# Fold products in groups of eight, and zero fills moved behind the first unit's fifth step

## The chip, the cores and the metric

One core of a Trainium2 chip runs the whole program. The metric is the device time of one execution in microseconds; the kernel before took 965.82 us (median of three runs, 963.59 to 968.89). TensorE, VectorE, ScalarE and GpSimd each work through their own list of instructions in order; SyncE issues most DMAs, GpSimd the zero fills and the indexed writes. In the profile they are PE (its weight loads PEld), DVE, ACT, POOL and SP.

## The reference

Three layers in a row on 2304 tokens of width 512.

```python
# attention, 4 batches x 8 heads, 576 tokens, 32 landmarks (means of 18 rows)
A = sm(q, k_lm); Bm = sm(q_lm, k_lm); C = sm(q_lm, k)
Z = Bm.T / (norm1(Bm) * norminf(Bm) + 1e-6)
for _ in range(6):
    Z = 2 * Z - Z @ Bm @ Z
x = (A @ Z @ C @ v)                      # then heads side by side: 2304 x 512
# dense layer, 512 -> 2048 -> 512
h = x @ w_in; g = h * tanh(softplus(h)); x = g @ w_out
# eight experts, 512 -> 1024 -> 512, the best two of each token
logits = x @ w_gate + softplus(x @ w_noise) * noise
for e in range(8):                       # weights: softmax over the token's two
    out[mask] += top2_w * (relu(x[mask] @ w1[e]) @ w2[e])
```

## The kernel before

The tokens go through in eight units of 288, two per batch of the attention. `w_in` is never multiplied by the attention's output itself: per batch, the 32 landmark rows of each of the eight heads (`WT`, 64 x 32 per head, the product of `Z`, `C` and `v`) are multiplied into `w_in` first, which gives a 256 x 2048 matrix. This is **the fold** (`fold`, lines 680 to 713). It works in four blocks `fb` of 512 columns. For each block and each half `hg` (four heads), four products with 64 rows of `w_in`, 32 columns of weights and 512 columns of output run on TensorE (line 700), each in a quarter of the output partitions of one bank of tag g. ScalarE then copies the bank to `gt` in the matmul format (line 707), and VectorE writes what the rounding left over (line 709), so that later products are made of three parts. `w_in` comes as 64-bit integers holding doubles; `conv_in` converts it (`widen`, lines 599 to 603) in batch 0 and stores the result, and `reload_in` loads it again for batches 1 to 3 into six `win` buffers.

**The dense layer** is 64 steps, `hidden(s)`, eight per unit: step s makes 256 hidden columns of unit s // 8. A hidden step is twelve products into the one `ps_h` buffer (line 733, tile `gt` of block (s % 8) // 2); ScalarE copies it out (line 746), then come a minimum on VectorE (753), four activations (755 to 761), a VectorE product (763), and the parts `gh` (ScalarE, 768) and `gl` (VectorE, 771). Then come the step's 24 down products (788 to 790) into the unit's four accumulators (tag acc, four banks in all). "Down step 16" below is the point at which the down products of steps 0 to 15 are through, that is, batch 0's two units. `conv_out` loads the 16 chunks of `w_out` into two alternating buffers, widens them (tiles `raw` and `t`, line 599 on) and splits each (660 on ScalarE, 662 on VectorE).

**The attention** of batch b (`attention`) begins when some steps of the batch before are through. It loads kT and qT for two groups of heads and v, reduces kT and qT to landmarks (line 327), iterates Z (548 to 556) and ends in the W products (568), which VectorE copies into `WT` (571).

**Routing** (`route`) follows each unit: ScalarE copies the accumulators to `yT` (839, one buffer), VectorE transposes them into `rr` (851, one buffer), TensorE makes the gate products (866), VectorE ranks the experts in some forty small instructions, and GpSimd scatters each token's row to its slots in HBM (1012). The slots of the first round are filled with zeros first: `zeros` writes a zero tile (812) and issues 24 fills from GpSimd's queue (282), in three zones of rows per expert (288, 288, 64): eight fills of 96 x 3 x 516 floats for either large zone, eight of 64 x 516 for the small one. Unit 0's `route` waits for zone 0 to be filled, unit 1's for zone 1, unit 2's for zone 2.

Last come **the experts**, in jobs of 384 or 256 slots: gather and transpose, 12 products up and three per block down, and an indexed add to `out` (1185).

**The order of the work** is made by a planner, `Order.run`. Each part of the kernel is a generator that asks for an engine, a buffer or an event. Whenever an engine is free in the planner's clock, the ready request with the smallest due time is written down as the next instruction of that engine, with costs given by hand:

```python
yield op("T", 1.06)      # one fold group, planned cost in us
yield wait(event); tk = yield get(ring, n)
```

So a wait in this code decides where later instructions stand; on the chip an instruction waits only for the data and the buffers that it touches.

Of the kernel before, what the change touches and what calls it, by code (L numbers as in the profile page):

```python
# [6 lines left out]
F32 = mybir.dt.float32  # L7
# [5 lines left out]
OP = mybir.AluOpType  # L13
# [5 lines left out]
LM, SEG = 32, 18  # L19
# [167 lines left out]
def op(engine, cost, late=0.0):  # L187
    return ("op", engine, cost, late)


def wait(event):
    return ("wait", event)


def get(ring, n=1):
    return ("get", ring, n)
# [18 lines left out]
class Kern:  # L215
# [76 lines left out]
    def attention(self, b):  # L292
# [249 lines left out]
        for it in range(6):  # L542
            tk = yield get(self.r_g)
# [25 lines left out]
        for a in range(2):  # L569
            yield op("V", 0.13)  # L570
            V.tensor_copy(
                WT.rearrange("p (g a) l -> p g a l", a=2)[:, :, a, :], w[a][:, : 2 * LM].rearrange("p (g l) -> p g l", g=2)
            )
# [106 lines left out]
    def fold(self):  # L680

        o, V, A, T = self.o, self.V, self.A, self.T
        for b in range(B):
            yield wait(self.got_WT[b])
            for fb in range(4):
# [3 lines left out]
                tw = {}  # L689
                for hg in range(2):  # L690
                    for c in (2 * hg, 2 * hg + 1):
                        yield wait(self.got_win[b, fb, c])
                        tw[c] = self.t_win[fb, c]
                    tk = yield get(self.r_g)
                    p = self.bank()
                    yield op("T", 1.06)
                    for h in range(4):
                        r = slice(64 * (h % 2), 64 * (h % 2) + 64)
                        c = 2 * hg + h // 2
                        T.matmul(  # L700
                            p[32 * h : 32 * h + 32, :], self.WT[b][r, c, :], self.win[fb, c][r].bitcast(F32),
                            start=True, stop=True,
                        )
                    for c in (2 * hg, 2 * hg + 1):
                        o.put(self.r_win, tw[c])
                    yield op("A", ca(512))
                    A.copy(gt[:, 0, hg, :], p)
                    yield op("V", cv(512))
                    V.tensor_tensor(out=gt[:, 1, hg, :], in0=p, in1=gt[:, 0, hg, :].bitcast(F32), op=OP.subtract)
                    o.put(self.r_g, tk)  # L710
# [94 lines left out]
    def zeros(self):  # L805


        yield wait(self.downed[2])
# [19 lines left out]
    def route(self, u, acc, ta):  # L828
# [28 lines left out]
        if u < len(self.filled):  # L857
            yield wait(self.filled[u])
# [557 lines left out]
def lay_out(q, k, v, moe_w_in, moe_w_out, moe2_w_gate, moe2_w_noise, moe2_noise, moe2_w1, moe2_w2):  # L1416
# [11 lines left out]
    wi = c(moe_w_in.reshape(4, 128, 4, 512).transpose(2, 0, 1, 3)).reshape(16, 128, 512).view(np.int64)  # L1428
# [27 lines left out]
```

## Time and profile before

| | |
|---|---|
| median of three runs | 965.82 us (963.59, 965.82, 968.89) |
| profiled execution: device time | 968.66 us |
| its span, first to last instruction | 966.8 us, 18134 instructions |
| mean granted TensorE clock | 0.984 |
| fold, line 700: TensorE | 34.2 us busy in 256 matmuls |
| zero fills of the slots: DMA issues | 16 of 580.5 KB, and eight small ones |

Each run is one execution; the profile is of a further one. Busy time of an engine is the time in which at least one of its instructions is in flight. Matmuls are pipelined, so rows of the timeline overlap: their starts tell the pace. A row's bracket says how long the engine had been idle before it, and whose end released it. A line number is that of the function that issued it; loads all go through line 287 and zero fills through 282, so for these the tile's name tells which it is.

### The profile page before, as it was taken

The numbers are of one execution on the slowest core, as the hardware profiler recorded it, in microseconds if no ns is written. First come the engines' busy times: TensorE is split into PE (matmuls) and PEld (weight loads), VectorE is DVE, ScalarE is ACT, GpSimd is POOL, SyncE is SP. The second block draws the span as 40 slices with busy tenths as digits, with TensorE's granted clock in tenths as the row PEclk, the third lists the DMA queues.
The fourth block names the chain that finished last, engine by engine and source line by source line (L and its number), as shares of the span: only waits on it lengthen the run. The fifth ranks groups of instructions, "written<-read, shape, count | busy, mean of one in ns | idle before, by whom it ended". The sixth has DMA issues, their size and how long they took to land. (4 is left out here: it accounts for less than half of the span.)

```text
span 966.8 us, 18134 instructions
## 1 busy us (share of the span) xinstructions
PE 914.0 (95%) x7135; PEld 799.1 (83%) x7135; DVE 625.7 (65%) x1519; ACT 457.6 (47%) x825; POOL 136.4 (14%) x129
## 2 busy tenths in 40 slices
PE   9979768999999998999999989999999999999995
PEld 7767656878886877889898979899989899999984
DVE  6999689566986669486958466646565555445411
ACT  2247655667766686588853233333333223323210
POOL 0002100223101200202020412101121011111102
PEclk9989989999999999999999999999999999999998
DMA  8677950565406410323243667666556355464103
GB/s 303 198 256 255 360 209 3 152 192 173 194 7 200 164 53 2 115 67 86 58 153 91 153 191 162 148 169 143 135 118 158 109 111 125 98 165 94 17 3 51
DMA packets 70075, 131.62 MB, mean 136 GB/s; under 512 B 13696, under 2 KB 34784, under 8 KB 69984
## 3 DMA queue, kind: packets, MB, share of 16 engines
q1 hardware_dynamic: 56960, 96.16, 32.6%
q0 software_dynamic: 13024, 34.25, 15.1%
q8 instruction: 58, 0.95, 0.4%
q14 instruction: 33, 0.27, 0.1%
HBM read 91.94 MB, written 39.48 MB: 136 GB/s over the span
## 5 line engine op out<-in xcount | busy, mean ns | idle before, releaser
L1151 PE MATMUL ps_up<-xh,mw 128*128 128x256 f32 (+1 forms) x1024 | 265.5, 312 | 2.8 <-ACT mw L1039 2.1
L1151 PEld LDWEIGHTS ps_up<-xh,mw 128*128 128x128 f32 x1024 | 183.1, 189 | 15.5 <-ACT mw L1039 2.5
L1160 ACT ACTIVATE gh<-ps_up 128x384 fp32r<-128x384 f32 (+1 forms) x128 | 56.1, 438 | 285.7 <-PE ps_acc L1173 161.6
L1162 DVE SCALAR_TENSOR_TENSOR gl<-ps_up,gh 128x384 fp32r<-128x384 f32 (+1 forms) x128 | 62.7, 490 | 170.1 <-ACT gh L1160 169.9
L788 PE MATMUL ps_acc<-gh,wo 128*128 128x288 f32 x512 | 159.2, 311 | 5.3 <-ACT gh L768 5.0
L1151 PE MATMUL ps_up<-xl,mw 128*128 128x384 f32 (+1 forms) x512 | 159.3, 311 | 0.0
L789 PE MATMUL ps_acc<-gl,wo 128*128 128x288 f32 x512 | 153.2, 299 | 2.8 <-DVE gl L771 2.8
L790 PE MATMUL ps_acc<-gh,wo 128*128 128x288 f32 x512 | 152.7, 298 | 0.2 <-DVE wo L662 0.2
L733 PE MATMUL ps_h<-ah,gt 128*128 128x288 f32 x512 | 127.3, 306 | 15.7 <-ACT mh L746 15.2
L1172 PE MATMUL ps_acc<-mw,gh 128*128 128x512 f32 x320 | 126.5, 395 | 0.0
L1173 PE MATMUL ps_acc<-mw,gh 128*128 128x512 f32 x320 | 126.4, 395 | 0.0
L1174 PE MATMUL ps_acc<-mw,gl 128*128 128x512 f32 x320 | 125.8, 393 | 0.0
L1185 POOL DMA_INDIRECT out<-yp,off x40 | 67.0, 1674 | 376.9 <-DVE yp L1181 278.3
L788 PEld LDWEIGHTS ps_acc<-gh,wo 128*128 128x128 f32 x512 | 97.9, 191 | 25.5 <-issue 13.2
L733 PEld LDWEIGHTS ps_h<-ah,gt 128*128 128x128 f32 x512 | 90.0, 191 | 32.5 <-ACT mh L746 21.5
L1151 PEld LDWEIGHTS ps_up<-xl,mw 128*128 128x128 f32 x512 | 96.7, 189 | 10.0
L789 PEld LDWEIGHTS ps_acc<-gl,wo 128*128 128x128 f32 x512 | 98.0, 191 | 3.8 <-DVE gl L771 3.8
L1041 DVE TENSOR_TENSOR mw<-mraw,mw 128x1024 fp32r<-128x1024 f32 x72 | 87.8, 1223 | 18.5 <-ACT mw L1039 17.9
L790 PEld LDWEIGHTS ps_acc<-gh,wo 128*128 128x128 f32 x512 | 97.9, 191 | 0.4 <-DVE wo L662 0.4
L1012 POOL DMA_INDIRECT slots<-rr,sl x48 | 47.7, 994 | 336.4 <-DVE rr L1008 319.4
L1039 ACT CAST mw<-mraw 128x1024 fp32r<-128x1024 f32 x72 | 74.6, 1042 | 3.4 <-DMA mraw<-in_ew 3.4
L733 PE MATMUL ps_h<-al,gt 128*128 128x288 f32 x256 | 76.0, 297 | 0.0
(189 smaller groups left out, 1384.9 us busy)
## 6 DMA issues: line engine op xcount, KB each, us to landing
mraw<-in_ew SPq DMA_DIRECT2D x72, 512.0 KB, 4.1
win<-win_d SPq DMA_DIRECT2D x48, 256.0 KB, 3.4
xg<-slots SPq DMA_DIRECT2D x160, 64.0 KB, 3.1
slots<-zero POOLq DMA_DIRECT2D x16, 580.5 KB, 20.0
raw<-in_w_in SPq DMA_DIRECT2D x16, 512.0 KB, 4.7
raw<-in_w_out SPq DMA_DIRECT2D x16, 512.0 KB, 6.3
kT<-in_kT SPq DMA_DIRECT2D x8, 576.0 KB, 6.9
qT<-in_qT SPq DMA_DIRECT2D x8, 576.0 KB, 7.3
```

The source lines that it names most:

```text
L733: T.matmul(hp[:, i, :U], gt[:, x, hg, n : n + 128], AT[y][:, hg, :], start=k == 0, stop=k == 5)
L788: T.matmul(acc[c][:, :U], hi[:, n], gh[:, i], start=f + i == 0, stop=False)
L789: T.matmul(acc[c][:, :U], hi[:, n], gl[:, i], start=False, stop=False)
L790: T.matmul(acc[c][:, :U], lo[:, n], gh[:, i], start=False, stop=f + i == NF - 1)
L1039: self.A.copy(w[:, 0], raw)
L1041: self.V.tensor_tensor(out=w[:, 1], in0=raw, in1=w[:, 0].bitcast(F32), op=OP.subtract)
L1151: T.matmul(h[:, :n], w[:, i, 128 * c : 128 * c + 128], x[j][:, c, :n], start=k == 0, stop=k == 11)
L1162: self.V.scalar_tensor_tensor(out=gl[:, :n], in0=hp[:, :n], scalar=0.0, in1=gh[:, :n].bitcast(F32), op0=OP.max, op1=OP.subtract)
L1172: T.matmul(a, g[0][:, n], w[:, 0, 512:], start=first, stop=False)
L1173: T.matmul(a, g[0][:, n], w[:, 1, 512:], start=False, stop=False)
L1174: T.matmul(a, g[1][:, n], w[:, 0, 512:], start=False, stop=last)
L1185: st = self.G.indirect_dma_start(out=self.out[:, :], out_offset=bass.IndirectOffsetOnAxis(ap=off[:, b : b + 1], axis=0), in_=y, in_offset= ...
```

## The change

- The fold takes both halves of a block together: eight products of 64 x 32 into two banks. Of half 1 the two row halves change places (`(h ^ hg) % 2`), so that over each 32 columns one product uses rows 0 to 63 and one rows 64 to 127. The planner's cost of the group is 1.15 instead of two times 1.06; a group waits for all four `win` chunks and for two banks of tag g.
- For this, `w_in` is laid out with the row halves of chunks 2 and 3 exchanged (on the host), and `WT` is filled by two copies of 128 partitions and four of 64 per batch instead of two.
- The zero fills begin when down step 5 is planned (`downed[4]`) instead of down step 3 (`downed[2]`).
- Unit 0's `route` waits until all 24 fills have been issued; units 1 and 2 wait for none.

```diff
--- before.py
+++ after.py
@@ -568,9 +568,11 @@
                     T.matmul(w[a][R[h], LM * hg : LM * hg + LM], X[H[h], hg, LM:], R5[H[h], hg, :], start=True, stop=True)
         for a in range(2):
             yield op("V", 0.13)
-            V.tensor_copy(
-                WT.rearrange("p (g a) l -> p g a l", a=2)[:, :, a, :], w[a][:, : 2 * LM].rearrange("p (g l) -> p g l", g=2)
-            )
+            V.tensor_copy(WT[:, a], w[a][:, :LM])
+
+            for h in range(2):
+                yield op("V", 0.1)
+                V.tensor_copy(WT[R[1 - h], 2 + a], w[a][R[h], LM : 2 * LM])
         o.put(self.r_g, tk, 2)
         o.set(self.got_WT[b])
         for hg in range(2):
@@ -687,27 +689,29 @@
                 self.t_gt[b, fb] = yield get(self.r_gt)
                 self.gt[b, fb] = gt = self.gp.tile([128, 2, 2, 512], F32R, name="gt", tag="gt", bufs=4)
                 tw = {}
-                for hg in range(2):
-                    for c in (2 * hg, 2 * hg + 1):
-                        yield wait(self.got_win[b, fb, c])
-                        tw[c] = self.t_win[fb, c]
-                    tk = yield get(self.r_g)
-                    p = self.bank()
-                    yield op("T", 1.06)
-                    for h in range(4):
-                        r = slice(64 * (h % 2), 64 * (h % 2) + 64)
+                for c in range(4):
+                    yield wait(self.got_win[b, fb, c])
+                    tw[c] = self.t_win[fb, c]
+                tk = yield get(self.r_g, 2)
+                p = [self.bank() for _ in range(2)]
+
+                yield op("T", 1.15)
+                for h in range(4):
+                    for hg in range(2):
+                        r = slice(64 * ((h ^ hg) % 2), 64 * ((h ^ hg) % 2) + 64)
                         c = 2 * hg + h // 2
                         T.matmul(
-                            p[32 * h : 32 * h + 32, :], self.WT[b][r, c, :], self.win[fb, c][r].bitcast(F32),
+                            p[hg][32 * h : 32 * h + 32, :], self.WT[b][r, c, :], self.win[fb, c][r].bitcast(F32),
                             start=True, stop=True,
                         )
-                    for c in (2 * hg, 2 * hg + 1):
-                        o.put(self.r_win, tw[c])
+                for c in range(4):
+                    o.put(self.r_win, tw[c])
+                for hg in range(2):
                     yield op("A", ca(512))
-                    A.copy(gt[:, 0, hg, :], p)
+                    A.copy(gt[:, 0, hg, :], p[hg])
                     yield op("V", cv(512))
-                    V.tensor_tensor(out=gt[:, 1, hg, :], in0=p, in1=gt[:, 0, hg, :].bitcast(F32), op=OP.subtract)
-                    o.put(self.r_g, tk)
+                    V.tensor_tensor(out=gt[:, 1, hg, :], in0=p[hg], in1=gt[:, 0, hg, :].bitcast(F32), op=OP.subtract)
+                    o.put(self.r_g, tk + hg)
                 o.set(self.got_gt[b, fb])
             o.put(self.r_wt, self.t_WT[b])
         o.set(self.folded)
@@ -805,7 +809,7 @@
     def zeros(self):
 
 
-        yield wait(self.downed[2])
+        yield wait(self.downed[4])
         tk = yield get(self.r_raw)
         zero = self.wp.tile([128, D + LW], F32, name="zero", tag="raw", bufs=2)
         yield op("V", 0.2)
@@ -854,8 +858,8 @@
         sent, rr, trr = Event(), [], []
         o.spawn(send(), due_hidden(8 * u + 7) + DU["send"])
         yield wait(self.routed[u - 1] if u else self.emptied)
-        if u < len(self.filled):
-            yield wait(self.filled[u])
+        if u == 0:
+            yield wait(self.filled[-1])
         tg = yield get(self.r_g)
         lg = self.bank()
         yield op("T", 0.9)
@@ -1425,7 +1429,10 @@
     vA = c(vh[:, :, :, :512].reshape(4, 2, 4, 4, 128, 64).transpose(0, 1, 4, 3, 2, 5)).reshape(8, 128, 1024)
     vB = c(vh[:, :, :, 512:].transpose(0, 1, 3, 2, 4)).reshape(8, 64, 256)
 
-    wi = c(moe_w_in.reshape(4, 128, 4, 512).transpose(2, 0, 1, 3)).reshape(16, 128, 512).view(np.int64)
+
+    wi = moe_w_in.reshape(4, 2, 64, 4, 512)
+    wi = np.concatenate([wi[:2], wi[2:, ::-1]], axis=0)
+    wi = c(wi.reshape(4, 128, 4, 512).transpose(2, 0, 1, 3)).reshape(16, 128, 512).view(np.int64)
     wo = c(moe_w_out.reshape(16, 128, 4, 4, 32).transpose(0, 1, 3, 2, 4)).reshape(16, 128, 512).view(np.int64)
 
     wgn = np.concatenate([moe2_w_gate, moe2_w_noise], axis=1).reshape(4, 4, 32, 16)
```

In the changed program the lines from the fold on stand three or four lower: 700 is 703, 733 is 737, 788 to 790 are 792 to 794, 812 is 816, 866 is 870.

What the planner makes of it at three places follows. First, TensorE at the end of batch 0's down products (down step 16). Line 700 is a fold group, 866 unit 1's gate products, 788 to 790 down products. Before, half 1 of block 2 of batch 1, behind which come unit 1's gate products:

```order
L789 MATMUL ps_acc<-gl,wo 128x288
L790 MATMUL ps_acc<-gh,wo 128x288
L700 MATMUL ps_g<-win,wt 32x512 x4
L866 MATMUL ps_g<-wgn,yT 32x16 x36
L788 MATMUL ps_acc<-gh,wo 128x288
L789 MATMUL ps_acc<-gl,wo 128x288
```

In the changed program the fold of block 2 (line 703) stands between hidden products, all down products up to step 16 being through:

```order
L737 MATMUL ps_h<-al,gt 128x288
L737 MATMUL ps_h<-ah,gt 128x288
L703 MATMUL ps_g<-win,wt 32x512 x8
L737 MATMUL ps_h<-ah,gt 128x288
L737 MATMUL ps_h<-al,gt 128x288
```

and 24 hidden products later the fold of block 3, then the gate products of unit 0:

```order
L737 MATMUL ps_h<-al,gt 128x288
L737 MATMUL ps_h<-ah,gt 128x288
L703 MATMUL ps_g<-win,wt 32x512 x8
L870 MATMUL ps_g<-wgn,yT 32x16 x36
L792 MATMUL ps_acc<-gh,wo 128x288
L793 MATMUL ps_acc<-gl,wo 128x288
```

Unit 0's gate products stood behind down step 8 before; now they stand behind down step 16, and behind the last two folds of batch 1. Hidden steps 20 and 21 stand between these folds, with no down product.

Second, TensorE at down step 32, where batch 2's hidden steps begin. Before, the two folds of block 0 (not shown) stand among the last down products, and a half of block 1 behind the first six hidden products:

```order
L789 MATMUL ps_acc<-gl,wo 128x288
L790 MATMUL ps_acc<-gh,wo 128x288
L733 MATMUL ps_h<-ah,gt 128x288
L733 MATMUL ps_h<-al,gt 128x288
L733 MATMUL ps_h<-ah,gt 128x288 x2
L733 MATMUL ps_h<-al,gt 128x288
L733 MATMUL ps_h<-ah,gt 128x288
L700 MATMUL ps_g<-win,wt 32x512 x4
L733 MATMUL ps_h<-ah,gt 128x288
L733 MATMUL ps_h<-al,gt 128x288
```

In the changed program the first fold of batch 2 comes behind the last down product:

```order
L792 MATMUL ps_acc<-gh,wo 128x288
L793 MATMUL ps_acc<-gl,wo 128x288
L794 MATMUL ps_acc<-gh,wo 128x288
L703 MATMUL ps_g<-win,wt 32x512 x8
L737 MATMUL ps_h<-ah,gt 128x288
L737 MATMUL ps_h<-al,gt 128x288
L737 MATMUL ps_h<-ah,gt 128x288 x2
L737 MATMUL ps_h<-al,gt 128x288
```

The fold of block 0 has moved from 18 and 30 products ahead of the last down product to just behind it, and the hidden products of the same block follow it at once.

Third, VectorE around the memset of the zero tile, line 812 before, 816 in the changed program. Before (771 writes `gl`, 753 is the minimum, 599 to 603 widen and 662 splits a chunk of `w_out`; eight chunks are split ahead of the memset):

```order
L603 SCALAR_TENSOR_TENSOR t<-raw,t 128x512
L603 SCALAR_TENSOR_TENSOR win<-raw,win 128x512
L771 SCALAR_TENSOR_TENSOR gl<-mh,gh 128x576
L812 MEMSET zero 128x516
L753 TENSOR_SCALAR me<-mh 128x576
L599 TENSOR_SCALAR raw<-raw 128x512
L662 TENSOR_TENSOR wo<-t,wo 128x512
L601 SCALAR_TENSOR_TENSOR raw<-raw 128x512
```

In the changed program (775 and 757, 601 to 605, 664):

```order
L757 TENSOR_SCALAR me<-mh 128x576
L601 TENSOR_SCALAR t<-raw 128x512
L603 SCALAR_TENSOR_TENSOR t<-raw,t 128x512
L816 MEMSET zero 128x516
L605 SCALAR_TENSOR_TENSOR t<-raw,t 128x512
L767 SCALAR_TENSOR_TENSOR mh<-me,mh 128x576
L664 TENSOR_TENSOR wo<-t,wo 128x512
L396 TENSOR_REDUCE mB<-ps_g 128x1
```

The memset has moved from behind the eighth chunk of `w_out` to behind the twelfth. On GpSimd the 24 fills now stand in one run ahead of unit 0's six scatters; before, fourteen came first, then four scatters, a fill, two scatters and the other nine.

## Rows read from the trace of the kernel before

**Rows 1.** The page, part 1: busy us, share of the span, instructions, by engine.

```profile
PE 914.0 (95%) x7135; PEld 799.1 (83%) x7135; DVE 625.7 (65%) x1519; ACT 457.6 (47%) x825; POOL 136.4 (14%) x129
```

**Rows 2.** Table by stretches: stretch, its length, busy us and instructions of PE, PEld, DVE, ACT, POOL; granted clock (1.00 full), DMA share, GB/s.

```profile
96.00:120.00 24.00, 17.93 (x151) 15.43 (x149) 16.45 (x30) 16.53 (x32) 4.00 (x6) 0.99 1.02 360
...
120.00:144.00 24.00, 14.19 (x100) 11.31 (x100) 19.67 (x41) 14.30 (x29) 0.00 (x0) 0.80 0.58 224
...
144.00:168.00 24.00, 19.75 (x333) 16.72 (x334) 22.91 (x68) 13.48 (x27) 0.00 (x0) 1.00 0.01 3
...
288.00:312.00 24.00, 21.91 (x245) 15.83 (x245) 14.45 (x29) 12.76 (x25) 5.58 (x6) 1.00 0.54 172
...
648.00:672.00 24.00, 24.00 (x153) 21.90 (x153) 14.35 (x36) 9.04 (x16) 4.65 (x3) 1.00 0.67 153
```

**Rows 3.** Timeline of VectorE: start us, us, engine, line, what [idle before <-releaser].

```profile
112.68 0.46 DVE L753 TENSOR_SCALAR me<-mh 128x576 f32<-128x576 f32 x1
...
118.77 0.43 DVE L599 TENSOR_SCALAR raw<-raw 128x512 int32<-128x512 int32 x1 [5.63 <-DMA raw<-in_w_out]
...
119.12 0.75 DVE L763 SCALAR_TENSOR_TENSOR mh<-me,mh 128x576 f32<-128x576 f32 x1
...
127.56 1.35 DVE L327 TENSOR_REDUCE kl<-kT 128x64 f32<-128x1152 f32 x1 [1.20 <-DMA kT<-in_kT]
...
131.15 1.35 DVE L327 TENSOR_REDUCE ql<-qT 128x64 f32<-128x1152 f32 x1 [1.64 <-DMA qT<-in_qT]
```

**Rows 4.** Timeline of ScalarE, same columns.

```profile
119.90 0.68 ACT L768 ACTIVATE gh<-mh 128x576 fp32r<-128x576 f32 x1 [5.11 <-DVE mh L763]
...
122.56 0.64 ACT L746 COPY mh<-ps_h 128x576 f32<-128x576 f32 x1
```

**Rows 5.** Timeline of TensorE in the head.

```profile
123.25 0.61 PE L733 MATMUL ps_h<-ah,gt 128*128 128x288 f32 x1 [7.77 <-ACT mh L746]
...
132.56 1.65 PE L356 MATMUL ps_g<-kT,ql 64*32 64x288 f32 x16 [4.50 <-DVE ql L327]
```

**Rows 6.** Timeline of SyncE's DMA issues.

```profile
108.52 0.33 SPq L287 DMA_DIRECT2D raw<-in_w_out  x1
...
112.68 2.42 SPq L287 DMA_DIRECT2D kT<-in_kT  x1
```

**Rows 7.** Timeline of GpSimd: the first eight fills, and the last before the scatters.

```profile
88.56 5.78 POOL L282 DMA_DIRECT2D slots<-zero  x8 [86.52 <-DVE me L753]
...
112.04 0.67 POOL L282 DMA_DIRECT2D slots<-zero  x1 [1.02 <-DMA slots<-zero]
```

**Rows 8.** DMA issues of 84 to 130 us: count, KB each, median us to landing.

```profile
slots<-zero POOLq DMA_DIRECT2D x14, 580.5 KB, 20.4
...
raw<-in_w_out SPq DMA_DIRECT2D x6, 512.0 KB, 11.1
```

**Rows 9.** Timeline of TensorE in the body: one fold group among down products.

```profile
176.99 0.29 PE L789 MATMUL ps_acc<-gl,wo 128*128 128x288 f32 x1
177.12 0.29 PE L790 MATMUL ps_acc<-gh,wo 128*128 128x288 f32 x1
177.34 1.06 PE L700 MATMUL ps_g<-win,wt 64*32 64x512 f32 x8
...
178.71 0.29 PE L790 MATMUL ps_acc<-gh,wo 128*128 128x288 f32 x1
```

**Rows 10.** Groups by line: form, count | busy us, mean ns of one | idle before.

```profile
L700 PE MATMUL ps_g<-win,wt 64*32 64x512 f32 x256 | 34.2, 601 | 0.0
...
L709 DVE TENSOR_TENSOR gt<-ps_g,gt 128x512 fp32r<-128x512 f32 x32 | 22.0, 688 | 15.0 <-ACT gt L707 14.7
...
L707 ACT CAST gt<-ps_g 128x512 fp32r<-128x512 f32 x32 | 18.5, 578 | 21.3 <-PE ps_g L700 21.3
```

**Rows 11.** Timeline of TensorE: the W products of batch 1.

```profile
172.41 0.45 PE L568 MATMUL ps_g<-R,X 32*64 32x32 f32 x16
```

**Rows 12.** Waits of TensorE, 168 to 216 us: us in total, times, longest.

```profile
PE ps_g L866 <- ACT yT L839: 1.9, 3, 0.6
```


## The prediction

> **What bounds the kernel now.** The page's busy times come first: TensorE is busy for 914.0 of 966.8 us, VectorE for 625.7 [rows 1]. Most of the span can only shrink if matmul work goes; the 52.8 us in which TensorE idles have to be found by stage. The table by stretches of 24 us shows where: from 96 to 168 us TensorE idles for 6.07 + 9.81 + 4.25 = 20.1 us, and its mean granted clock falls to 0.80 in one stretch; in the body, 288 to 312 us idles for 2.09, and a stretch of the expert stage for nothing [rows 2]. The reader is to see two regimes: a head (batch 0, and the attention of batch 1) that something else limits, and a body that TensorE limits.
>
> In the head, VectorE works its instructions in order. At 118.77 it had sat for 5.63 us until a w_out transfer landed; ScalarE's next step then had waited 5.11 us for VectorE, and TensorE's next hidden step 7.77 us for ScalarE's copy out of its only ps_h buffer [rows 3 to 5]. Later kT and qT of batch 1 came late as well: 1.20 and 1.64 us on VectorE, 4.50 us on TensorE [rows 3, 5]. That w_out load had been issued at 108.52, ten microseconds before, and the kT load at 112.68 [rows 6]. From 88.56 to 112.04 GpSimd had issued fourteen zero fills [rows 7]; a fill took a median 20.4 us to land in that time, a w_out load 11.1 us [rows 8], with the DMA engines at a share of 1.02 [rows 2]. So the head's idle time is, for the larger part, loads that share the DMA engines with fills.
>
> **The fold.** Removed: 32 groups of four products, two per block; added: 16 groups of eight. What a group costs is read from the body, where TensorE is full: products start every 0.13 us, and the third product after the group starts at 178.71 instead of 177.12 + 3 x 0.133 = 177.52. That is 1.19 us [rows 9]. The eight matmuls of a group (two passes of four) last 0.601 us each [rows 10], yet the group spans 1.06 us [rows 9]: four run at once, and the second pass starts 1.06 - 0.60 = 0.46 us after the first. If eight run at once, a group has eight more starts; sixteen small matmuls span 0.45 us [rows 11], so a start takes at most 0.03 us, and I add 0.08 for what shows at the end: 1.27 us. A pair saves 2.38 - 1.27 = 1.11 us. The twelve blocks of batches 1 to 3 lie in the body: **12 x 1.11 = 13.3 us**. The four of batch 0 I cost at nothing, for VectorE is the bound there; if that cover is gone they add 4.4.
>
> No row shows products of both row halves going on together over the same 32 columns. The bounds are 1.19 us (nothing added) and 1.19 + 2 x 0.46 = 2.11 us (the halves in turn, two more passes). I take 1.27, since the row nearest to it, the group of four, has both row halves busy at once and writing one bank. The Trainium skill, "TensorEngine Tiling (Array Packing)", section "Restrictions and Gotchas", says under PSUM pressure that different row tiles cannot access the same PSUM bank at the same time. By that rule the group of before would have needed four passes, some 2.0 us; it took 1.06, so the trace does not agree, and what the rule would make of the change (two groups in turn) is a rival below, with a small chance.
>
> The copies of WT grow from two to six per batch, between the W products and the fold; in batch 1 eighteen products (2.4 us) stand between on TensorE, in the other batches more work. Cost 0; if that cover is gone, under 1 us per batch.
>
> **What the longer group uncovers.** It takes both g banks, and a block's fold now stands in one place. At down step 16 the order puts hidden steps 20 and 21 straight behind the fold of block 2, then the fold of block 3, then unit 0's gate products (moved there from down step 8), then down products into banks that unit 1's yT copies have yet to free. Behind a fold come, for each half, ScalarE's copy, 0.578 us, and VectorE's subtraction, 0.688 [rows 10]: the last low half is ready after 0.58 + 0.69 + 0.69 = 1.96 us, while the six hidden products (0.8 us) can start from 0.58 on; 1.4 us idle. The next step waits for the ps_h copy, 0.64 [rows 4]. The gate products wait for a bank, 0.58 + 0.69 = 1.27. The first yT copy costs one of the three waits, 0.6 each, that this place has now [rows 12]. Sum 3.9, against 1.9 now: 2.0 us more. At down step 32 the order has no down product left when batch 2's first fold comes: 1.4 + 0.64 again; then the chain from a hidden step to its down products (copy 0.64, minimum 0.46, four ScalarE steps of 0.68, 0.75, 0.68: 5.2 us [rows 3, 4]) has only 0.64 + 0.8 + 1.19 + 0.8 = 3.4 us beside it: 1.8 idle. Sum 3.8, against 2.1 now [rows 2]: 1.7 more. Together **3.7 us lost**. Below: 0, if other work fills in; above: double, since ScalarE and VectorE have other instructions queued.
>
> **The fills.** Their first instruction, a memset on VectorE, moves from behind the eighth split of w_out to behind the twelfth, about 20 us of VectorE work. All 24 fills then go out in one run: 16 x 0.594 + 8 x 0.132 = 10.6 MB where 14 x 0.594 = 8.3 MB do now; at the 360 GB/s of 96 to 120 us that is 29 us [rows 2, 8]. Loads 9 to 14 of w_out and the first kT and qT of batch 1 get clear of them; loads 15 and 16, the second kT and qT and the v loads do not. Of the 5.63 + 1.20 + 1.64 = 8.5 us that VectorE waits for late loads [rows 3] I take 5 as recovered; bounds: all 8.5, or more lost than now. Unit 0's gate work leaves VectorE's queue between 144 and 168 us, where VectorE is busy for 22.91 of 24 and TensorE idles for 4.25 [rows 2]: I take 2. Against it, batch 1's W products stand half a hidden and half a down step earlier in the order, so 18 products, 2.4 us, are still to do. **Head: 5 + 2 - 2.4 = 4.6 us gained.**
>
> The wait of the first scatter: on GpSimd unit 0's scatters queue behind 24 fills, and behind them stand five fills of out and unit 1's scatters. Unit 0's gate products now run at down step 16, far more than 29 us after the memset, so I cost the wait at 0; if the fills were not done, unit 1's transposes into rr (one buffer) would wait, on VectorE.
>
> **Sum.** 13.3 - 3.7 + 4.6 = 14.2 us. The profiled execution took 968.66 us (span 966.8): 954.5. It lies 2.84 above the median 965.82 of the three runs; against the median that is 951.6, so **952 us**.
>
> **Rivals.**
> - The head gets all of it: loads wait for nothing (8.5), and the borders cost half (1.9). For: the loads issued before the new memset are those that stall VectorE longest now. Against: four kinds of load still meet the fills. 13.3 - 1.9 + 8.5 + 2 - 2.4 = 19.5, so 946 us.
> - The change doesn't do what it says: the row halves take turns. For: no row shows two halves over the same columns. Against: the four of now, in both halves, don't. Saved 12 x (2.38 - 2.11) = 3.2; each of the two borders waits 0.84 longer: 3.2 - 3.7 - 1.7 + 4.6 = 2.4, so 963 us. The skill's rule on banks would give this time too.
> - Slower: the run of 24 fills falls on batch 1's loads. The second kT and qT go out some 3 us after the first fill and are wanted about 13 us after it; if they land only with the fills, 29 us after the start, VectorE waits some 14 us, and v and the last w_out load add 8: 22 instead of 8.5. For: kT was issued at 112.68 and VectorE could begin on it at 127.56, with fills under way [rows 3, 6]. Against: loads and fills share, and these landed in 15 us. 13.3 - 3.7 - 13.5 - 2.4 = -6.3, so 972 us. It decides from the point at which the head loses over 14 us, that is, if batch 1's W products (at 172.41 now [rows 11]) come after about 186.
>
> **How the numbers follow.** Forecast 0.56, all recovered 0.20, halves in turn 0.11, fills on the loads 0.13. A measurement here tells about 0.5%, 4.8 us, from no change. Faster by more: 0.50 + 0.20 + 0.02 of the first three, 0.72. Same: 0.05 + 0.08 + 0.02 of the first, third and fourth, 0.15. Slower: 0.01 + 0.01 + 0.11 of the same, 0.13. The range runs from 941, where the second case takes batch 0's 4.4 as well, to 968, past the halves in turn; it leaves out the slower case and the tails.
>
> **What would show it.** A fold group of sixteen matmuls that spans 1.1 to 1.3 us (2 us: halves in turn). The memset at 105 to 110 us, no VectorE wait of 5 us on w_out, batch 1's W products at 160 to 170 us. TensorE idle for 1 to 2 us behind the folds at down steps 16 and 32. Wrong would be: W products past 172 us, or borders that idle for over 4 us each more than now.

## The result and the profile after

The changed kernel took **978.91 us** (median of four runs, 976.97 to 983.68) where the kernel before took 965.05 on the same chip: **1.0145** of its time, 95% interval 1.0097 to 1.0193. The forecast was 952 us (941 to 968), faster. The profiled execution took 978.09 us, its span is 976.0.

The page of the changed kernel, part 1 [rows 1]:

```profile
PE 916.3 (94%) x7156; PEld 809.0 (83%) x7156; DVE 628.5 (64%) x1535; ACT 458.6 (47%) x825; POOL 136.4 (14%) x129
```

TensorE's busy time did not fall, though the fold was shortened. Its table by stretches, with 192 to 216 us and the whole stretch 168 to 528 us added [rows 2]:

```profile
96.00:120.00 24.00, 21.25 (x160) 17.71 (x160) 22.68 (x42) 18.74 (x35) 6.46 (x10) 0.93 0.79 265
120.00:144.00 24.00, 16.62 (x163) 12.83 (x163) 19.23 (x52) 15.26 (x33) 6.01 (x10) 0.93 1.00 329
144.00:168.00 24.00, 21.98 (x282) 18.29 (x282) 19.51 (x44) 15.78 (x28) 2.70 (x6) 1.00 0.44 109
192.00:216.00 24.00, 17.81 (x164) 14.95 (x165) 10.26 (x38) 10.57 (x22) 0.00 (x0) 0.72 0.53 185
288.00:312.00 24.00, 20.82 (x192) 15.78 (x184) 12.25 (x55) 8.34 (x17) 5.84 (x6) 0.86 0.32 96
...
168.00:528.00 360.00, 335.04 (x3291) 297.17 (x3290) 255.50 (x711) 237.12 (x438) 46.69 (x48) 0.96 0.33 104
```

and that last stretch in the kernel before:

```profile
168.00:528.00 360.00, 348.70 (x3348) 301.72 (x3348) 260.36 (x713) 241.39 (x446) 51.59 (x58) 1.00 0.36 115
```

The head is better: from 96 to 168 us TensorE idles for 72 - 59.85 = 12.2 us, not 20.1. The body is worse: TensorE idles for 25.0 us of 360, not 11.3, and its granted clock is 0.96, not 1.00.

**The fold.** TensorE in the body, the products around a group [rows 9]:

```profile
177.82 0.29 PE L794 MATMUL ps_acc<-gh,wo 128*128 128x288 f32 x1
178.04 1.09 PE L703 MATMUL ps_g<-win,wt 64*32 64x512 f32 x16
179.06 0.40 PE L792 MATMUL ps_acc<-gh,wo 128*128 128x288 f32 x1
...
179.44 0.30 PE L794 MATMUL ps_acc<-gh,wo 128*128 128x288 f32 x1
```

Sixteen matmuls span 1.09 us where eight spanned 1.06: eight products do run side by side.

**The head.** VectorE (the memset, the longest wait on w_out), GpSimd (first eight and last fill), TensorE (W products of batch 1), in this order [rows 3, 7, 11]:

```profile
106.52 0.49 DVE L816 MEMSET zero<- 128x516 f32 x1
...
127.81 0.43 DVE L601 TENSOR_SCALAR raw<-raw 128x512 int32<-128x512 int32 x1 [4.18 <-DMA raw<-in_w_out]
```

```profile
107.33 5.58 POOL L282 DMA_DIRECT2D slots<-zero  x8 [105.28 <-DVE zero L816]
...
156.29 0.53 POOL L282 DMA_DIRECT2D slots<-zero  x1 [1.18 <-DMA slots<-zero]
```

```profile
162.53 0.45 PE L568 MATMUL ps_g<-R,X 32*64 32x32 f32 x16
```

The W products come at 162.53 instead of 172.41: 9.9 us earlier. Not all of that is the change's. In a second profile of the kernel before (the run `before_again` below) they come at 168.29, so the gain lies between 5.8 and 9.9 us:

```profile
168.29 0.45 PE L568 MATMUL ps_g<-R,X 32*64 32x32 f32 x16
```

**Down step 16.** TensorE from the fold of block 2 on, and ScalarE at the same place:

```profile
189.59 1.09 PE L703 MATMUL ps_g<-win,wt 64*32 64x512 f32 x16
194.53 0.61 PE L737 MATMUL ps_h<-ah,gt 128*128 128x288 f32 x1 [3.85 <-ACT gt L711]
...
198.94 0.61 PE L737 MATMUL ps_h<-ah,gt 128*128 128x288 f32 x1 [0.73 <-ACT mh L750]
...
202.12 1.96 PE L703 MATMUL ps_g<-win,wt 64*32 64x512 f32 x16
205.58 0.95 PE L870 MATMUL ps_g<-wgn,yT 128*32 128x16 f32 x72 [1.50 <-DVE gt L713]
207.89 0.61 PE L792 MATMUL ps_acc<-gh,wo 128*128 128x288 f32 x1 [1.36 <-ACT yT L843]
```

```profile
190.60 0.68 ACT L772 ACTIVATE gh<-mh 128x576 fp32r<-128x576 f32 x1 [0.27 <-DVE mh L767]
191.19 0.67 ACT L759 ACTIVATE me<-me 128x576 f32<-128x576 f32 x1
...
193.32 0.68 ACT L765 ACTIVATE me<-me 128x576 f32<-128x576 f32 x1
193.91 1.05 ACT L711 CAST gt<-ps_g 128x512 fp32r<-128x512 f32 x2
```

No down product starts between 188.58 and 207.89. The copy of the folded block starts at 193.91, 3.2 us after the fold has ended: ScalarE has `gh` and four activations of a hidden step ahead of it in its list. After that idle stretch the products last 0.44 us and not 0.29, and the next fold spans 1.96 and not 1.09. The table by stretches shows why: the granted clock is at its lower level (0.50) from 194.2 to 204.2 us, and once more from 207.9 to 211.1, after the waits of 1.50 and 1.36 us.

```profile
190.70:194.00 3.30, 0.00 (x0) 0.00 (x0) 0.99 (x2) 3.20 (x6) 0.00 (x0) 1.00 0.67 205
194.20:204.20 10.00, 8.75 (x40) 6.05 (x40) 3.01 (x5) 4.14 (x7) 0.00 (x0) 0.50 0.11 34
204.40:207.70 3.30, 0.95 (x72) 0.85 (x72) 1.61 (x4) 1.71 (x6) 0.00 (x0) 1.00 0.82 239
207.90:211.10 3.20, 3.20 (x15) 3.16 (x15) 2.68 (x17) 0.83 (x3) 0.00 (x0) 0.50 0.98 361
```

### The profile page after: what moved, and what is told of

It reads as the page before. It is cut to its first block, busy times and chain, and to the rows that moved or that the text cites. A ratio compares the mean times of both kernels' runs of the same rounds, so it can differ in the third digit from the quotient of the medians.

```text
span 976.0 us, 18224 instructions
## 1 busy us (share of the span) xinstructions
PE 916.3 (94%) x7156; PEld 809.0 (83%) x7156; DVE 628.5 (64%) x1535; ACT 458.6 (47%) x825; POOL 136.4 (14%) x129
## 5 line engine op out<-in xcount | busy, mean ns | idle before, releaser
L737 PE MATMUL ps_h<-ah,gt 128*128 128x288 f32 x512 | 134.8, 322 | 14.0 <-ACT mh L750 7.7
L737 PEld LDWEIGHTS ps_h<-ah,gt 128*128 128x128 f32 x512 | 94.7, 201 | 32.1 <-ACT mh L750 12.9
L737 PE MATMUL ps_h<-al,gt 128*128 128x288 f32 x256 | 79.1, 309 | 0.0
## 6 DMA issues: line engine op xcount, KB each, us to landing
slots<-zero POOLq DMA_DIRECT2D x16, 580.5 KB, 20.1
```

Of the source, the lines that this page charges most:

```text
L737: T.matmul(hp[:, i, :U], gt[:, x, hg, n : n + 128], AT[y][:, hg, :], start=k == 0, stop=k == 5)
```

## The experiments

Five sets of runs were made, each with the kernel before on the same chip. Before took 966 to 968 us in the second and third set and 979 in the first, fourth and fifth, so ratios are given, and positions in time are compared only between sets in which before took the same time. What makes the 1.3% between sets is not known: the first and the third set ran on a chip of the same number (7). The fold alone is the only kernel measured at both levels, and its two ratios agree (1.0089 and 1.0104). "Down step 8" and "64" are places counted in TensorE's timeline; from step 64 to the end every kernel takes 455 to 462 us.

**First set: the parts of the change.** The theory: the fold gains, and what loses is the wait for all fills ahead of unit 0's gate products. One rival: the fold in one place loses. The other: the planner's due times (the table `DU`) fit the order of before, so any move of the order loses about 1%.

The fold alone (the hunks of `zeros`, `route` undone):

```diff
-        yield wait(self.downed[4])
+        yield wait(self.downed[2])
...
-        if u == 0:
-            yield wait(self.filled[-1])
+        if u < len(self.filled):
+            yield wait(self.filled[u])
```

> The eight-wide fold alone, fills and the waits for them as before. Theory (the planner's wait of unit 0's gate products for all fills makes the loss; the fold itself gains): the gate products of unit 0 stand behind down step 8 again, no stop of the down products of over 6 us at down step 16; 948 to 960 us against 965 before. Rival (the fold group in one place makes the loss, by the stalls behind it at the batch borders): 970 to 980 us. Second rival (the due times fit the order of before, and any move of it costs about 1%): 970 to 980 us.

Measured: **1.0089** (1.0067 to 1.0111). Repeated in the third set:

> The fold alone once more (the change's fold, the fills as before), to have its profile beside the next three and, by its ratio, beside the block of eight in two turns (1.018) and the fold planned at 2.12 us (1.013). Theory 'block' (planning the fold as one block of eight costs about 17 us, in the loads of batch 0 before down step 8 and in TensorE's waits in the expert steps, and the products side by side give about 9 back): 1.007 to 1.011 again, down step 8 reached 4 to 8 us later than in the kernel before (137 us), the stretch from down step 8 to 64 some 8 to 14 us longer than its 366. Rival (any order costs about 1%, and the first reading was of that): 0.998 to 1.006.

**1.0104** (1.0065 to 1.0144); down step 8 at 146 us, from there to 64 it took 371 (366 before), 5 more where 8 to 14 were expected. So the fold alone loses too, as both rivals had it.

The fills alone (the hunks of the fold, `WT` and `w_in` undone, the other two kept):

> The fold of before; fills from down step 5 on, and unit 0's gate products wait for all of them. Theory: the stop of the down products at down step 16 is there (gate products of unit 0 behind hidden step 22), 12 us or more against 4.4 before; head some 8 us faster; no gain from the fold: 970 to 985 us. Rival (fold in one place): no loss, 957 to 966 us. Second rival (any move): 970 to 980 us.

**1.0255** (1.0232 to 1.0278).

The change, with the wait for all fills moved to just ahead of unit 0's scatters:

```diff
-        if u == 0:
-            yield wait(self.filled[-1])
         tg = yield get(self.r_g)
...
+        if u == 0:
+            yield wait(self.filled[-1])
```

> The whole change, but unit 0 waits for the fills right before its scatters and not before its gate products. Theory: gate products of unit 0 at down step 8, no long stop at down step 16, head as fast as with the change: 942 to 955 us. Rival (fold in one place): 968 to 980 us. Second rival: 968 to 980 us.

**1.0077** (1.0060 to 1.0093). And with each unit waiting for its own zone, as before:

> The whole change, but units 0, 1 and 2 wait for one zone each as before, in front of their gate products. Theory: unit 0's gate products stand at down step 11, before unit 1's accumulators are wanted, so no long stop at down step 16: 945 to 958 us. Rival (fold in one place): 968 to 980 us. Second rival: 968 to 980 us.

**1.0073** (1.0048 to 1.0098). Each is under the 1.0145 of the change (1.0097 to 1.0193), though only just by the intervals, and none is under 1: the theory is half right at most.

**Second set: what the fold loses by.** `before_again` is the kernel before:

> The kernel before once more, for a profile on the chip that runs the next three. All theories: ratio to before 1.000, its five-eighths of the expert stage from the first unit's last step to the last unit as on the first chip, TensorE idle 9 to 14 us between 168 and 528 us.

1.0007 (0.9991 to 1.0022). It reaches down step 8 at 137 us and 64 at 503, where the first profile of the same kernel has 142 and 507.

Only the planner's cost of a fold group changed:

```diff
-                    yield op("T", 1.06)
+                    yield op("T", 1.08)
```

> Only the planner's cost of a fold group of four products is changed, from 1.06 to 1.08 us, so that a few steps from the second batch's end on are issued in another order; nothing is computed otherwise. Theory 'order' (the due times fit the order of before, and what the order loses is decided by which waits it happens to open): 0.997 to 1.008. Theory 'both banks at once' (the loss is that a block of eight takes both PSUM banks of the small products and that its two evictions come together): 0.998 to 1.002, since the block is as before.

**1.0023** (1.0006 to 1.0040): the order by itself moves the time, here a little.

The fold alone, planned at 2.12 us:

```diff
-                yield op("T", 1.15)
+                yield op("T", 2.12)
```

> The fold of eight as in the change, the fills as before, but the planner counts 2.12 us for it, as for two groups of four, instead of 1.15; so it plans the rest at the pace of before. Theory 'order': the rest comes out nearer to the order of before, and the ratio with it, 0.988 to 1.002. Theory 'both banks at once': the block still takes both banks, 1.005 to 1.012, as the fold alone (1.009) did.

**1.0133** (1.0104 to 1.0163). A cost nearer to the old one did not bring the old time back; in that form "order" failed. "Both banks" expected up to 1.012 and was not told apart from a badly fitted order.

The order of the fold alone, its eight products in two turns:

```diff
-                V.tensor_copy(WT[R[1 - h], 2 + a], w[a][R[h], LM : 2 * LM])
+                V.tensor_copy(WT[R[h], 2 + a], w[a][R[h], LM : 2 * LM])
...
-                for h in range(4):
-                    for hg in range(2):
-                        r = slice(64 * ((h ^ hg) % 2), 64 * ((h ^ hg) % 2) + 64)
+                for hg in range(2):
+                    for h in range(4):
+                        r = slice(64 * (h % 2), 64 * (h % 2) + 64)
...
-    wi = moe_w_in.reshape(4, 2, 64, 4, 512)
-    wi = np.concatenate([wi[:2], wi[2:, ::-1]], axis=0)
+    wi = moe_w_in
```

> The order of the run with the fold alone, instruction for instruction, but the eight products of a block in two groups of four that follow each other on TensorE, rows as before (no swap of the halves in w_in): the block spans 2.0 to 2.2 us instead of 1.09, 16 blocks, 13 of them behind the first units. If TensorE's time counts in that order: ratio 1.018 to 1.024 (1.009 of the fold alone and 13 us more of 966). If what TensorE saves there only makes it wait longer for ScalarE and VectorE (theory 'order' and theory 'both banks at once' alike): 1.007 to 1.013.

**1.0182** (1.0156 to 1.0207). Its group in the body:

```profile
298.06 1.92 PE L703 MATMUL ps_g<-win,wt 64*32 64x512 f32 x16
299.91 0.40 PE L792 MATMUL ps_acc<-gh,wo 128*128 128x288 f32 x1
```

The next product starts 1.85 us after the group's start, not 1.02: 0.83 us more per block. The two readings of the fold alone lie 0.8 and 0.9% under it, 7.5 to 9 us; so the side-by-side fold gains here, and the fold in one block, in two turns as before, takes 17 us more than before did. Whether that is its order or the two banks that it takes at once, these runs do not separate.

**Third set: the fills with the old fold, and new due times.** Fills from down step 4 on, zone waits:

```diff
-        yield wait(self.downed[2])
+        yield wait(self.downed[4])
```

> The fold as before (two groups of four), the fills from down step 4 on, and each of the first units waits for its own zone alone, as before. Theory 'parts' (the start of the fills frees 7 to 10 us ahead of down step 8, and only the wait for all of them ahead of the gate products gives it back): down step 8 at 126 to 131 us, ratio 0.988 to 0.997. Rival 'due times' (whatever comes earlier is waited off by an order that was fitted to the fills as they were): down step 8 early, but ratio 0.999 to 1.008, the stretch from down step 8 to 64 longer by as much.

**1.0178** (1.0137 to 1.0220). Down step 8 came at 146 us, not at 126 to 131 and later than the 137 of before, although the memset moved from 85.7 to 99.6: with the old fold the later fills gain nothing in the head. 64 came at 525. Both theories missed. The trace shows what went wrong in the head. The first fill (GpSimd), two loads of w_out (SyncE) and VectorE's wait for w_out:

```profile
100.40 6.77 POOL L282 DMA_DIRECT2D slots<-zero  x9 [98.36 <-DVE zero L812]
```

```profile
103.58 0.33 SPq L287 DMA_DIRECT2D raw<-in_w_out  x1
106.19 3.06 SPq L287 DMA_DIRECT2D raw<-in_w_out  x1
```

```profile
117.35 0.43 DVE L599 TENSOR_SCALAR raw<-raw 128x512 int32<-128x512 int32 x1 [9.73 <-DMA raw<-in_w_out]
```

These loads were issued behind the first fill, and VectorE waited 9.73 us, longer than the 5.63 of before. In the change, three loads of w_out go out at 99.95, 104.94 and 107.58, ahead of the first fill or with it. So later fills help only where the order puts the loads ahead of them.

With the wait for all fills ahead of the scatters:

> The fold as before, the fills from down step 4 on, the first unit waits for all of them, but only ahead of its scatters and not ahead of its gate products. Beside the fills of the change alone (1.0255), which differ in the place of that wait only. Theory 'parts': 0.990 to 1.000, at least 2.5% under it. Rival 'due times': 1.003 to 1.012. If the place of the wait were not what costs: 1.020 to 1.028.

**1.0253** (1.0207 to 1.0299), as with that wait ahead of the gate products (1.0255). With the old fold the place of the wait is not what costs, so the first set's theory falls for it.

The change with zone waits, and other due times. They were found by letting the planner try many values and keeping those whose plan ends earliest in its own costs:

```diff
-    w7=0.03, t0=145.6, t1=9, t2=4.8, m0=566.3, win=67.3, wo=4.1, att=84.6, grp=73, sof=-40.6, fet=191.2, fev=157.4,
+    w7=0.03, t0=145.6, t1=9, t2=4.8, m0=566.3, win=32.8, wo=-57.1, att=191.1, grp=132.0, sof=-82.6, fet=204.8, fev=91.5,
...
```

> The change with each zone waited for by its own unit (1.007 on its chip), and the due times of the planner chosen anew for it; the computation and every instruction are the same, in another order. Theory 'due times': 0.985 to 1.000, since the fold's and the head's gain are no longer waited off. Theory 'block' (the block of eight costs in itself): 1.003 to 1.015.

**0.9985** (0.9965 to 1.0006), against 1.0073 with the old due times. Down step 8 came late, at 154, and yet 64 at 506 (503 before): 352 us for those steps. TensorE's table for it, and then for the old fold with late fills and zone waits, idle for 16.4 and 19.7 us of 360:

```profile
168.00:528.00 360.00, 343.65 (x3415) 305.40 (x3406) 268.78 (x739) 246.30 (x455) 52.97 (x59) 0.99 0.36 115
```

```profile
168.00:528.00 360.00, 340.29 (x3316) 290.82 (x3317) 251.52 (x698) 237.90 (x439) 53.38 (x60) 0.98 0.36 112
```

**Fourth set: due times for each kernel.** The edit is the table `DU` alone, as above. The change itself:

> The change itself, no instruction added or taken away, with the planner's due times chosen anew for it; the wait for all the fills still stands ahead of the first gate products. Theory 'due times' (the change loses because its costs no longer fit due times that were chosen for the order before): under the change's 1.0145, by 0.5 to 1.5%, so 1.000 to 1.010, with unit 0's gate products still behind the fills. Theory 'the change costs in itself' (the block of eight, the late fills): 1.010 to 1.025.

**1.0049** (1.0027 to 1.0070), under its 1.0145: 981.77 us where before took 978.55. The kernel before:

> The kernel before, no instruction added or taken away, with due times chosen anew in the same way. The control for the three others: if new due times gain by themselves, it is 0.975 to 0.995, and what the others gain is not the fold's or the fills'. If the due times of before are already fitted to it on the chip (theory 'due times'): 0.997 to 1.012.

**0.9911** (0.9880 to 0.9942), 970.40 us: its own due times were not the best either. So with due times chosen anew for both, in one set, the change as it stands is still 1.2% slower than the kernel before. Two more choices for the change with zone waits, the second in full:

> As the run with due times chosen anew (0.9985) with another choice, in which the loads of w_out come earlier: the first choice reached down step 8 at 154 us, the change at 135, but ran the steps from 8 to 64 in 352 us, the change in 381 and the kernel before in 366. Theory 'due times': the two gains can be had together, down step 8 at 132 to 142 us, the steps from 8 to 64 in 352 to 368, ratio 0.978 to 0.995. Rival (an early start is waited off later, whatever the due times): 0.997 to 1.010.

**1.0050** (1.0023 to 1.0077). Down step 8 at 130 us, 64 only at 526: this order's early start was waited off, as the rival had it. TensorE idles for 37 us of 360 and the clock is 0.95:

```profile
168.00:528.00 360.00, 322.81 (x3204) 281.35 (x3193) 246.73 (x687) 229.21 (x422) 53.71 (x60) 0.95 0.35 112
```

```diff
+    w7=0.03, t0=145.6, t1=9, t2=4.8, m0=566.3, win=-25.6, wo=-24.3, att=223.4, grp=167.9, sof=-74.4, fet=479.2, fev=144.4,
+    mkU=440.3, fold=-21.7, up=-28.1, down=44.0, mish=113.0, route=14.6, r6=328.5, r7=-228.3, send=26.2, rows=-302.2,
+    sc=138.4, sc6=868.6, yT=-13.8, rein=-18.2, rl=-285.7, zero=-234.9, w=0, lists=-114.1, wts=-15.5, spl=-442.3,
+    gath=503.8, turn=-225.0, fin=-192.8, part=69.6, mish2=-151.7, mdown=174.2, st1=0, st2=0, st3=2,
```

> A third choice of due times, the same instructions again: the loads of w_out less early, the W products of batch 1 planned about a quarter of a unit sooner than in the second. Theory 'due times': 0.980 to 0.998. Rival: 0.997 to 1.010. The three choices side by side show how far the order alone moves the time of one and the same set of instructions.

**0.9851** (0.9806 to 0.9896): 963.16 us, where the second choice took 983.46 in the same set. The same instructions under four tables of due times: 1.0073, 0.9985, 1.0050, 0.9851. (Only the number of small products that keep TensorE busy at the start differs; the last of them starts before 65 us.)

**Fifth set: the fold in the best order.** The best run again:

> The third choice of due times once more, beside the one before. Its gain is of the kernel if it shows on another set of executions: 0.980 to 0.992. Rival (it was of that chip, on which the kernel before took 979 us and not 966): 0.993 to 1.000.

**0.9872** (0.9852 to 0.9891): 966.82 us where before took 978.92. It was a set in which before takes 979 again, so whether the gain is as large where before takes 966 was not shown. The same order with the fold in two turns (diff as above):

> The fastest order so far (the third choice of due times, 0.985), instruction for instruction, but the eight products of a block in two turns of four, as in the run that did this to the fold alone. If the fold side by side is worth in this order what it was there (1.018 against 1.009 to 1.010): 0.8 to 1.0% over the repeat of the third choice, 0.993 to 0.996. Rival (in this order TensorE's time is covered by its waits): within 0.3% of the repeat. If all 16 x 1.0 us count: 1.6% over it.

**0.9985** (0.9965 to 1.0004): 977.13 us, above the 0.993 to 0.996 expected. The page and a group, side by side first, then in two turns, where TensorE is busy for 16.5 us more:

```profile
PE 901.3 (94%) x7109; PEld 798.6 (83%) x7109; DVE 629.4 (65%) x1535; ACT 457.0 (48%) x825; POOL 135.4 (14%) x129
```

```profile
286.30 1.09 PE L703 MATMUL ps_g<-win,wt 64*32 64x512 f32 x16
287.31 0.40 PE L792 MATMUL ps_acc<-gh,wo 128*128 128x288 f32 x1
```

```profile
PE 917.8 (94%) x7109; PEld 806.2 (83%) x7109; DVE 629.4 (65%) x1535; ACT 458.2 (47%) x825; POOL 134.9 (14%) x129
```

```profile
284.85 1.92 PE L703 MATMUL ps_g<-win,wt 64*32 64x512 f32 x16
286.70 0.41 PE L792 MATMUL ps_acc<-gh,wo 128*128 128x288 f32 x1
```

0.84 us more per block, 13.4 for the sixteen; the time grew by 977.13 - 966.82 = 10.3. Most of TensorE's time counts in this order, but not all. In the two profiles (961.1 and 972.3 us) 2.6 us of the difference come ahead of down step 8, 7.3 from there to 64 and 1.3 behind. That the twelve blocks of batches 1 to 3 would make 10.1 by themselves is chance.

## Why the prediction was wrong

**The fold: right.** I took 1.27 us for a group of eight. By the same reckoning it is 179.44 - (177.82 + 3 x 0.133) = 1.22, so a pair saves 2.38 - 1.22 = 1.16 and twelve blocks 13.9 us (forecast 13.3) where TensorE is full and its clock is not down. The Trainium skill's rule that different row tiles cannot access the same bank at once ("TensorEngine Tiling (Array Packing)", "Restrictions and Gotchas") would have had the eight take turns, as in the run where they do and span 1.92 us; they spanned 1.09, so the trace does not agree. Against the fold in two turns, in an order that suits it, the products side by side were worth 10.3 us of time over all sixteen blocks; that run tests 0.84 of the 1.16 us per block.

**The head: right in this order, and not by the fills alone.** Forecast 4.6; the W products came 5.8 to 9.9 earlier, in the stated range of 160 to 170. The memset stood where I put it, the longest wait on w_out was 4.18 us. But the fills took about 50 us, from 107.33 until past 156.29, not 29: after the first eight, each issue waits for a fill to land. And with the old fold the same later fills brought a longer wait on w_out, since loads stood behind them. That fills ahead of loads delay them is borne out; that a later memset clears the loads depends on the order, and the forecast was lucky there.

**Down step 32: right in size for the waits, without the clock.** TensorE's waits there, forecast 3.8:

```profile
301.48 0.40 PE L737 MATMUL ps_h<-ah,gt 128*128 128x288 f32 x1 [0.78 <-ACT gt L711]
...
302.20 0.55 PE L737 MATMUL ps_h<-ah,gt 128*128 128x288 f32 x2 [0.19 <-DVE gt L713]
...
303.34 0.85 PE L737 MATMUL ps_h<-ah,gt 128*128 128x288 f32 x2 [0.47 <-DVE gt L713]
...
306.12 0.61 PE L737 MATMUL ps_h<-ah,gt 128*128 128x288 f32 x1 [0.73 <-ACT mh L750]
...
312.30 0.40 PE L792 MATMUL ps_acc<-gh,wo 128*128 128x288 f32 x1 [1.31 <-ACT gh L772]
313.10 0.40 PE L793 MATMUL ps_acc<-gl,wo 128*128 128x288 f32 x1 [0.39 <-DVE gl L775]
```

They sum to 3.9. But the clock fell here too. After the first three of these waits, none over 0.78 us, it is at its lower level, and the next fold spans 1.96 us:

```profile
303.50:310.00 6.50, 5.77 (x30) 3.48 (x31) 1.01 (x2) 3.41 (x6) 4.84 (x6) 0.50 0.65 202
```

```profile
307.85 1.96 PE L703 MATMUL ps_g<-win,wt 64*32 64x512 f32 x16
```

**The step that failed: "Together 3.7 us lost", taken for the whole price of the new order.** At down step 16 I put 3.9 us of idle time; it was 3.85 + 0.73 + 1.50 + 1.36 = 7.4, 5.5 more than the 1.9 of before, where over 4 more was my sign of being wrong. I had let ScalarE copy the block as soon as it was folded; its list had five instructions ahead. The Trainium skill, "TensorEngine Tiling (Array Packing)", "PSUM Bottleneck", says that after a fourfold TensorE speedup the copy out of PSUM may become the bottleneck. Here TensorE waited 3.85 us for that copy, though for its place in ScalarE's list and not for its length (1.05 us for both halves). With the 1.8 us more at down step 32 the two borders lost 7.3 us, twice the forecast and just the upper bound given with it. The lower clock behind these waits had no term in the sum.

More than that, I priced two places and put the rest of the dense layer's steps at nothing. From the W products of batch 1 to down step 64 the change takes 353.2 us, the two profiles of the kernel before take 334.9 and 334.6. That is some 18 us lost, where the fold should have gained 13.9: some 32 to account for. Between 168 and 528 us TensorE idles for 25.0 - 11.3 = 13.7 us more. The two borders have 7.3 of them; among the rest are waits for VectorE in the attention of batches 2 and 3:

```profile
280.96 0.37 PE L548 MATMUL ps_g<-XB 32*32 32x96 f32 x8 [2.00 <-DVE XB L493]
...
358.79 1.18 PE L356 MATMUL ps_g<-kT,ql 64*32 64x288 f32 x16 [2.61 <-DVE ql L327]
```

A clock lower by 0.04 over 360 us is about 14; this is an estimate from the two tables, and a high one, since it counts idle time as well. At least 4 us I can't place. "A body that TensorE limits" was true of the order of before, in which TensorE waits 11 us; in the order of the change the same work waits 25.

**The rivals.** None came true. The nearest in time, 972 us, would have come with W products after 186. The right one was missing: the edits cost little, the planner's new order costs much.

**What is shown, and what not.** That the order and not the instructions carries the loss is shown by order alone. The change with zone waits has the instructions of the change in another order; under four tables of due times it takes 1.0073, 0.9985, 1.0050 and 0.9851 of the time before, the last two 2% apart in one set. In sets where before took 965 and 968, the change took 978.91 us and the first new table 965.96. Which place in the order costs how much is read from single traces, and no run tests it. That the loss comes of due times *fitted* to before is not shown: new ones gained 0.9% for the kernel before as well. Nor is it shown how much of the 1.3 to 1.5% of the best version is the change's and how much new due times', since they were chosen anew for each; against the kernel before with new due times, in the same set, its 963.16 us are 0.7% under 970.40. And the 963 to 967 us of its two sets lie within 0.5% of the 966 to 968 that the kernel before takes in others. Why the later fills lose in the body too with the old fold (378 us from down step 8 to 64, 366 before), and how much the wait for all fills costs under new due times, stays open.

## What to carry to other kernels

Where a planner writes the order, an edit has two prices: what its instructions cost, and what the new order does everywhere else; here the first was forecast within 1 us and the second was more than twice as large, with the other sign. So choose the due times anew before judging an edit, do the same for the kernel before as a control, and measure the edit itself with the order held fixed (the fold in two turns, instruction for instruction). When one engine's work shrinks, look at which instructions stand ahead of its consumer in the consumer's own list: freed time on TensorE became idle time behind ScalarE, and the products behind that idle time ran at the lower clock.

## What the runs showed of the hardware

Eight products of 64 x 32 over 512 columns, two banks, both row halves over the same 32 output partitions: 1.09 us, with the next product 1.02 us after the start; in two turns 1.92 and 1.85 us. After an idle stretch of 3.85 us TensorE's granted clock was at the lower of its two levels from 194.2 to 204.2 us, with products paced at 0.24 us instead of 0.13. After three waits of 0.78, 0.19 and 0.47 us between 300.70 and 303.34 it was there as well, from 303.5 to 310.0. The kernel before took 966 to 968 us in some sets and 979 in others, 1.3% apart, and both on a chip numbered 7; positions and times of kernels can be compared within one set, or between sets in which before took the same.
